# A Nyström attention with two expert layers: C v per head, blocks of 512 in the second layer, attention steps spaced

## The chip, the cores and the metric

The program runs on one core of a Trainium2 chip, in one launch. The metric is device time in microseconds. The core has five engines that run side by side, each with its own queue of instructions: PE (TensorE, matrix products), DVE (VectorE), ACT (ScalarE), POOL (GpSimd), and SP (SyncE), which here only issues DMAs. An instruction waits in its queue until the semaphores it names are set, and everything behind it on that engine waits with it.

## The reference

```
for the 8 heads of each of 4 batches (S = 576 tokens, 64 columns, m = 32 landmarks):
    q_lm, k_lm = means of 18 neighbouring tokens
    A  = softmax(q k_lm^T / 8);  Bm = softmax(q_lm k_lm^T / 8);  C = softmax(q_lm k^T / 8)
    Z  = Bm^T / (norm1(Bm) * norminf(Bm) + 1e-6)
    six times:  Z = 2 Z - Z Bm Z
    attn = A Z C v
x = attn as (2304 tokens, 512)
h = x @ w_in   (512 x 2048);  g = h * sigmoid(h);        x = g @ w_out   (layer 1)
h = x @ w_in2;                g = h * tanh(log1p(e^h));  out = g @ w_out2  (layer 2)
```

## The kernel before

**Products.** Nearly every product of the two layers is made of three matmuls on operands that are split into a high and a low part: high times high, high times low, low times high.

**Attention.** The 8 heads of a batch go in two groups of 4 heads; a group of a batch is a unit, and there are 8 units. In a unit, `cp` (line 356) transposes C by PE, `nb` gives the norms, and `cv` (line 372) is C v. Six tiles of 96 tokens are summed; for each there are two matmuls, one for a pair of heads, of 64 rows of C by 128 columns of v. So a pair computes C of either head times v of either head, and half of the result is of no use. The useful half is picked on DVE: `s2r` (line 388) is a mask times the scale, `vt` (390) takes one 64-column half, and `rv` (391) adds the other. Then six Newton rounds follow (`nw`, line 421, with `rv` and `rb` evictions). At last `u` (line 524) gives the attention's output times layer 1's weights, in eight column tiles of 32 side by side, and `uw` (541, 544) splits it.

**Opening, 0 to about 181 us.** The attention of batches 0 and 1 and the blocks 0 and 1 of layer 1 (`ha`, `ya`) are put in order by a planner, which is given a cost on an engine for each step (`Step([("pe", 1.6)])`).

**Layer 1, about 181 to 470 us.** The 2304 tokens are 8 blocks of 288, the 2048 hidden columns are 16 tiles. Step t = 16 i + j computes `h` of tile j (6 matmuls), its silu on ACT, DVE and POOL, and, two steps late, `y` of step t-2 (12 matmuls into four banks). At the turn of two blocks, four evictions `yo` (687 on ACT, 689 on DVE) free the four banks for the next block's first `y`. The attention of batches 2 and 3 is fed in as a background generator by `advance()`, called twice a step with 1.35 credits. The weights of layer 2 are converted in the background too (`rawt`, `ct`, lines 593 to 600). Here the framework's scheduler sets the order.

**Layer 2, about 470 to 886 us.** 6 blocks of 384 tokens, 16 steps each, in the order written (`manual_schedule` for ACT, DVE and PE). Step t runs `hh` (12 matmuls of 384 columns), the mish of it, and the out products of step t-2: `o` (line 1106), 3 chunks of 128 tokens by 3 matmuls of 512 columns. `hh` has three banks, `o` the other five. The mish is, on DVE, `e`, `n`, `e`, then `z` three times; on ACT two exponentials, a logarithm and the cast to the high part `g`; on POOL the low part `g` (1050). After a block's last out product `out_block` (1064 to 1077) negates each chunk into a buffer `ot`, of which there are three, and SP stores it by two DMAs. All evictions are on ACT, except in the last block.

## Time and profile before

| what | value |
|---|---|
| median of 3 runs | 889.91 us (886.08, 889.91, 894.31) |
| profiled execution | 887.88 us, its span 886.1 us |
| PE busy | 851.9 us, 96% of the span |
| DVE, ACT, POOL busy | 648.5, 475.5, 290.3 us |
| mean granted PE clock | 0.983 of full speed |

The span is the time from the first to the last instruction that the profiler saw; the profiled execution's own time has 1.8 us more around it. Busy shares are means over all stages. A row of the timeline is a run of instructions of one kind, with the idle time just before it and what ended that in brackets. PE's matmuls overlap one another, so the row of a single matmul is longer than the distance between two starts; distances between starts are the price of one.

### The profile page before, as it was taken

How to read it: one execution, taken by the hardware profiler on the slowest of the kernel's cores; microseconds unless marked ns; L12 is line 12 of the kernel's file. 1: busy time of each engine (PE TensorE's matmuls, PEld its weight loads, DVE VectorE, ACT ScalarE, POOL GpSimd, SP SyncE). 2: the span in 40 equal slices, each digit the busy share in tenths (PEclk: the TensorE clock that was granted, in tenths of full speed). 3: DMA queues.
4: the chain of work that ended last, by engine and by line, in shares of the span. 5: the costliest groups of instructions: out<-in, count | busy, mean ns of one | idle time of the engine just before them, and what ended most of it. 6: DMA issues, size and time to landing. Idle time of an engine off the chain costs nothing.

```text
span 886.1 us, 15069 instructions
## 1 busy us (share of the span) xinstructions
PE 851.9 (96%) x5424; PEld 740.1 (84%) x5424; DVE 648.5 (73%) x1289; ACT 475.5 (54%) x1045; POOL 290.3 (33%) x331
## 2 busy tenths in 40 slices
PE   6889999999999898999999999999999999999997
PEld 5656777769998797889899889999998998998996
DVE  3878878778586868743565987787787787787776
ACT  4657555355445555654565555555555455555543
POOL 1311323034433446534333432232242242242221
PEclk8779999999999999999999999999999999999999
DMA  8735475344363466812551111000110110000000
GB/s 229 200 98 147 155 211 155 70 125 97 97 141 116 115 212 221 274 52 73 171 169 56 51 27 26 20 28 18 27 27 12 34 28 5 32 1 1 36 1 36
DMA packets 95355, 79.63 MB, mean 90 GB/s; under 512 B 52528, under 2 KB 80688, under 8 KB 95280
## 3 DMA queue, kind: packets, MB, share of 16 engines
q1 hardware_dynamic: 95280, 78.67, 30.8%
q8 instruction: 42, 0.69, 0.3%
q14 instruction: 33, 0.27, 0.1%
HBM read 60.82 MB, written 17.83 MB: 89 GB/s over the span
## 4 chain that ended last, share of the span: by engine, by line
PE 74%; DVE 8%; issue 5%; POOL 4%; ACT 4%; DMA 3%; SPq 1%; POOLq 0%; DVEq 0%; ACTq 0%
PE hh L609 21%; PE o L1106 21%; PE y L609 11%; PE h L609 5%; PE ya L835 5%; PE ha L635 4%; POOL g L667 2%; PE u L524 2%; DMA q<-in_q_dram 2%; PE nw L421 2%; DVE z L1044 1%; PE cv L372 1%; DVE rawt L596 1%; POOL rawt L591 1%; SPq L201 1%
## 5 line engine op out<-in xcount | busy, mean ns | idle before, releaser
L1050 POOL TENSOR_TENSOR g<-z,g 128x384 fp32r<-128x384 f32 x94 | 95.9, 1020 | 258.8 <-ACT g L1047 256.5
L1106 PE MATMUL o<-wh,g 128*128 128x512 f32 x576 | 166.3, 396 | 2.7 <-ACT g L1047 1.5
L609 PE MATMUL y<-g,wh 128*128 128x288 f32 x768 | 163.0, 302 | 5.6 <-POOL g L667 1.8
L609 PEld LDWEIGHTS y<-g,wh 128*128 128x128 f32 x768 | 124.5, 190 | 15.2 <-ACT th L664 4.1
L667 POOL TENSOR_TENSOR g<-g,g 128x288 fp32r<-128x288 f32 x96 | 81.2, 846 | 169.6 <-ACT g L666 140.3
L609 PE MATMUL hh<-yh,wi2h 128*128 128x384 f32 x384 | 130.4, 339 | 0.0
L609 PE MATMUL hh<-yh,wi2l 128*128 128x384 f32 x384 | 129.6, 338 | 0.0
L609 PE MATMUL hh<-yl,wi2h 128*128 128x384 f32 x384 | 129.5, 337 | 0.0
L1106 PEld LDWEIGHTS o<-wh,g 128*128 128x128 f32 x576 | 106.4, 188 | 23.5 <-ACT g L1047 3.7
L1047 ACT CAST g<-z 128x384 fp32r<-128x384 f32 x96 | 49.3, 514 | 132.2 <-DVE z L1046 132.2
L609 PE MATMUL y<-g,wl 128*128 128x288 f32 x384 | 114.0, 297 | 0.0
L1033 DVE TENSOR_SCALAR e<-hh 128x384 f32<-128x384 f32 x96 | 53.5, 557 | 69.3 <-PE hh L609 69.1
L609 PE MATMUL h<-ath,uw 128*128 128x288 f32 x384 | 95.2, 302 | 1.1 <-DVE uw L544 1.1
L1106 PE MATMUL o<-wl,g 128*128 128x512 f32 x288 | 82.2, 393 | 0.0
L1034 ACT ACTIVATE e<-e 128x384 f32<-128x384 f32 x96 | 50.3, 524 | 55.2 <-DVE e L1033 54.7
L665 DVE SCALAR_TENSOR_TENSOR g<-th,h 128x288 f32<-128x288 f32 x96 | 42.9, 447 | 50.4 <-ACT th L664 48.1
L609 PEld LDWEIGHTS hh<-yh,wi2h 128*128 128x128 f32 x384 | 72.1, 188 | 4.1
L609 PEld LDWEIGHTS hh<-yl,wi2h 128*128 128x128 f32 x384 | 72.1, 188 | 3.9
L609 PEld LDWEIGHTS y<-g,wl 128*128 128x128 f32 x384 | 72.7, 189 | 0.4 <-issue 0.4
L609 PEld LDWEIGHTS h<-ath,uw 128*128 128x128 f32 x384 | 67.4, 189 | 5.8 <-issue 3.6
L1044 DVE SCALAR_TENSOR_TENSOR z<-z,r 128x384 f32<-128x384 f32 x96 | 69.8, 727 | 3.3
L609 PEld LDWEIGHTS hh<-yh,wi2l 128*128 128x128 f32 x384 | 72.0, 188 | 0.0
(163 smaller groups left out, 1591.7 us busy)
## 6 DMA issues: line engine op xcount, KB each, us to landing
rawi<-in_moe_w_in_dram SPq DMA_DIRECT2D x16, 512.0 KB, 4.9
rawo<-in_moe_w_out_dram SPq DMA_DIRECT2D x16, 512.0 KB, 3.6
rawt<-in_moe_w_in_dram SPq DMA_DIRECT2D x16, 512.0 KB, 4.8
w2c<-ct SPq DMA_DIRECT2D x32, 256.0 KB, 2.6
rawt<-in_moe_w_out_dram SPq DMA_DIRECT2D x16, 512.0 KB, 4.4
w2r<-w2c SPq DMA_DIRECT2D x32, 256.0 KB, 2.8
v<-in_v_dram SPq DMA_DIRECT2D x32, 144.0 KB, 2.9
ysc<-yo SPq DMA_DIRECT2D x32, 144.0 KB, 1.8
```

Of the source, the lines that this page charges most:

```text
L421: pe.matmul(nbk[:, i, a : w + D], lhs, rv[:, i, a:], start=True, stop=True)
L609: pe.matmul(o, a, b_, start=first and i == 0, stop=last and i == n - 1)
L635: pe.matmul(hb[:, :HB], uw[j // 2][:, g, j % 2], ath[0][:, g, hf * HB : (hf + 1) * HB], start=g == 0, stop=g == 1)
L665: dve.scalar_tensor_tensor(g2, th, 1.0, hb[:, :HB], op0=ALU.add, op1=ALU.mult)
L667: eng.tensor_tensor(gl, g2, gh.bitcast(F32), op=ALU.subtract)
L835: pe.matmul(yb[hf, m][:, :HB], wof[j][:, m * P : (m + 1) * P], gst[j // 2][:, j % 2, hf], start=j == 0, stop=j == NF - 1,)
L1033: dve.tensor_scalar(e, h, 20.0, None, op0=ALU.min)
L1034: ins = act.activation(e, e, AF.Exp)
L1044: dve.scalar_tensor_tensor(z, z, -2.0, r, op0=ALU.add, op1=ALU.mult)
L1047: act.copy(gh, z)
L1050: eng.tensor_tensor(gl, z, gh.bitcast(F32), op=ALU.subtract)
L1106: pe.matmul(obank[i][c], a[:, c * P : (c + 1) * P], w, start=j == 0 and k == 0, stop=j == NF - 1 and k == 2,)
```

## The change

Three things are changed. First, `cv` is computed per head, in four column tiles of 32 that stand side by side: 24 matmuls of 64 columns in place of 12 of 128, and one DVE instruction scales the result into `rv`. `s2r`, `vt` and the mask `sel2` with its 5 POOL memsets are gone; the planner's costs for the two steps are lowered. Second, layer 2 goes in five blocks, three of 512 tokens and two of 384; a block of 512 has four chunks. `ot` has two buffers, and where there are four chunks the evictions alternate between ACT and DVE. At j = 0 the out products go chunk by chunk. Larger buffers (`BIG`) make some others move: `g` of layer 2 into other buffers, and 14 of the 16 low tiles of layer 2's input weights in pairs into the buffers of layer 1's weights. Third, `advance()` issues at most one step on PE at a call, keeps no more than 4 credits, and gives no credit away for a step without cost; at a turn of two blocks of layer 1 the first of the two calls is left out and the second, after `y`, gets twice the credits.

```diff
-NB2 = 384
+NB2 = (512, 512, 512, 384, 384)
+BIG = max(NB2)
...
-        yield Step([("pe", 1.6)], ...
+        yield Step([("pe", 1.2)], ...
...
         for r in range(S // PT):
-            for p in range(2):
+            for h in range(4):
                 pe.matmul(
-                    cv[64 * p : 64 * p + 64, :P].rearrange("a (h d) -> a h d", h=2),
-                    ct[r // 3][:, r % 3, 64 * p : 64 * p + 64],
-                    st["v", p][:, :, r, :],
+                    cv[32 * h : 32 * h + 32, :D],
+                    ct[r // 3][:, r % 3, 32 * h : 32 * h + 32],
+                    st["v", h // 2][:, h % 2, r, :],
                     start=r == 0,
                     stop=r == S // PT - 1,
                 )
-        yield Step([("dve", 2.1)])
+        yield Step([("dve", 1.6)])
...
-        s2r = ap.tile([P, 2], F32, tag="s2r", bufs=2, name=f"s2r{u}")
-        dve.tensor_scalar(s2r, sel2, rc[:, 1:2], n2[:, 3:4], op0=ALU.mult, op1=ALU.mult)
-        vt = ap.tile([P, D], F32, tag="lk", bufs=2, name=f"vt{u}")
-        dve.tensor_scalar(vt, cv[:, :D], s2r[:, 0:1], None, op0=ALU.mult)
-        dve.scalar_tensor_tensor(rv[:, i, -D:], cv[:, D:P], s2r[:, 1:2], vt, op0=ALU.mult, op1=ALU.add)
+        dve.tensor_scalar(rv[:, i, -D:], cv[:, :D], rc[:, 1:2], n2[:, 3:4], op0=ALU.mult, op1=ALU.mult)
...
-    def advance(n=1.0):
-        credit[0] += n
-        while credit[0] >= 1:
-            credit[0] -= 1
-            while bg:
-                try:
-                    next(bg[0])
-                    break
-                except StopIteration:
-                    bg.pop(0)
+    pend = {}
+
+    def advance(n=1.0, all=False):
+
+        credit[0] = min(credit[0] + n, 4.0)
+        begun = False
+        while bg and (credit[0] >= 1 or all):
+            gen = bg[0]
+            if gen not in pend:
+                pend[gen] = next(gen, None)
+            step = pend.pop(gen)
+            if step is None:
+                bg.pop(0)
+                continue
+            on_pe = bool(step.cost) and step.cost[0][0] == "pe"
+            if on_pe and begun and not all:
+                pend[gen] = step
+                break
+            pend[gen] = next(gen, None)
+            if step.cost:
+                credit[0] -= 1
+                begun = True
+            if on_pe and not all:
+                break
...
-                    if j < 11:
+                    if j < 2:
                         lo = pl.tile([P, ND, P], F32R, tag=f"lo{j}", name=f"wi2l{j}")
                     else:
-                        lo = wp.tile([P, ND, P], F32R, tag=f"g{j - 11}", name=f"wi2l{j}")
+                        if j % 2 == 0:
+                            los = wp.tile([P, 2, ND, P], F32R, tag=f"g{j // 2 - 1}", name=f"wi2l{j}")
+                        lo = los[:, j % 2]
...
-        advance(RB)
+        turn = t > LAG and (j - LAG) % NF in (NF - 1, 0)
+        if not turn:
+            advance(RB)
...
         if t >= LAG:
             emit_y(t - LAG)
-        advance(RB)
+        advance(2 * RB if turn else RB)
...
     def out_block(i):
-        for c in range(NCH):
-            ot = m2.tile([P, DM], F32, tag="ot", bufs=3, name=f"ot{i}_{c}")
-            if i < nblk - 1 or c == 0:
+        for c in range(NB2[i] // P):
+            ot = m2.tile([P, DM], F32, tag="ot", bufs=2, name=f"ot{i}_{c}")
+            if c == 0 or i < nblk - 1 and c == 2:
                 act.mul(ot, obank[i][c], -1.0)
-            elif c == 1:
+            elif c == 1 or i < nblk - 1:
                 dve.tensor_scalar(ot, obank[i][c], -1.0, None, op0=ALU.mult)
...
+        chunks = NB2[i] // P
         if j == 0:
-            obank[i] = [bank((NCH * i + c + 4) % 5, f"o{i}_{c}") for c in range(NCH)]
-        order = [(c, k) for k in range(3) for c in range(NCH)]
+            obank[i] = [bank((sum(NB2[:i]) // P + c + 4) % 5, f"o{i}_{c}") for c in range(chunks)]
+        order = [(c, k) for k in range(3) for c in range(chunks)]
+        if j == 0:
+            order = [(c, k) for c in range(chunks) for k in range(3)]
```

DVE in layer 1, where the attention of batch 2 and the conversion of weights meet (`uw` splits the attention's product, `rawt` and `ct` are weights, `g` the silu, `lm` the landmarks). Before:

```order
L286 TENSOR_REDUCE lm_3574<-qT_3575 128x32
L596 SCALAR_TENSOR_TENSOR rawt_3848<-rawt_3848 128x512
L596 SCALAR_TENSOR_TENSOR rawt_3957<-rawt_3957 128x512
L665 SCALAR_TENSOR_TENSOR g_3406<-th_3405,h_3397 128x288
L600 SCALAR_TENSOR_TENSOR ct_4104<-rawt_3848 128x512
L544 TENSOR_TENSOR uw_5_3421<-u_3411,uw_5_3421 128x256
L544 TENSOR_TENSOR uw_5_3421<-u_3412,uw_5_3421 128x256
```

Now:

```order
L285 TENSOR_REDUCE lm_3740<-qT_3741 128x32
L539 TENSOR_TENSOR uw_6_3534<-u_3524,uw_6_3534 128x256
L539 TENSOR_TENSOR uw_6_3534<-u_3525,uw_6_3534 128x256
L591 SCALAR_TENSOR_TENSOR rawt_4111<-rawt_4111 128x512
L591 SCALAR_TENSOR_TENSOR rawt_4239<-rawt_4239 128x512
L660 SCALAR_TENSOR_TENSOR g_3566<-th_3565,h_3557 128x288
```

The `uw` pair stands ahead of the two `rawt`, no longer behind them and `ct`.

PE at the turn from block 4 to block 5 of layer 1 (`y_3` ends the old block, `y_0` opens the new one). Before:

```order
L609 MATMUL y_3_3296<-g_288_3879,wl_14_1828 128x288
L609 MATMUL h_3992<-ath_2153,uw_1_3022 128x288
L609 MATMUL h_3992<-atl_2154,uw_1_3022 128x288
L609 MATMUL h_3992<-ath_2153,uw_1_3022 128x288 x2
L609 MATMUL h_3992<-atl_2154,uw_1_3022 128x288
L609 MATMUL h_3992<-ath_2153,uw_1_3022 128x288
L356 MATMUL cp_4007<-ident,ce_3842 96x128 x3
L609 MATMUL y_0_4011<-g_288_3917,wh_0_1522 128x288 x2
```

Now:

```order
L604 MATMUL y_3_3293<-g_288_3896,wl_14_1856 128x288
L604 MATMUL h_4023<-ath_2165,uw_1_3037 128x288
L604 MATMUL h_4023<-atl_2166,uw_1_3037 128x288
L604 MATMUL h_4023<-ath_2165,uw_1_3037 128x288 x2
L604 MATMUL h_4023<-atl_2166,uw_1_3037 128x288
L604 MATMUL h_4023<-ath_2165,uw_1_3037 128x288
L604 MATMUL y_0_4037<-g_288_3933,wh_0_1566 128x288 x2
```

The attention's `cp` no longer stands between `h` and the new block's first `y`.

ACT at the first turn of two blocks in layer 2, with the semaphores that each instruction waits for (DMAHW is a DMA, the others are engines). Before:

```order
L1041 ACTIVATE r_6521<-r_6521 128x384 [waits Activation_49]
L1069 ACTIVATE ot_0_6544<-o_0_5932 128x512 [waits PE_49]
L1069 ACTIVATE ot_1_6548<-o_1_5933 128x512 [waits DMAHW0_49,PE_49]
L1069 ACTIVATE ot_2_6552<-o_2_5934 128x512 [waits DMAHW3_49,PE_49]
L1034 ACTIVATE e_6569<-e_6569 128x384 [waits DVE_49]
```

Now, ACT and then DVE at the same turn:

```order
L1060 ACTIVATE r_6618<-r_6618 128x512 [waits Activation_49]
L1088 ACTIVATE ot_0_6644<-o_0_5983 128x512 [waits DMAHW0_49,PE_49]
L1088 ACTIVATE ot_2_6652<-o_2_5985 128x512 [waits DMAHW4_49,DMAHW5_49,PE_49,Activation_49]
L1053 ACTIVATE e_6673<-e_6673 128x512 [waits DVE_49]
```

```order
L1058 TENSOR_TENSOR e_6616<-n_6617,hh_6603 128x512 [waits DVE_49]
L1090 TENSOR_SCALAR ot_1_6648<-o_1_5984 128x512 [waits DMAHW3_49,PE_49]
L1090 TENSOR_SCALAR ot_3_6656<-o_3_5986 128x512 [waits DMAHW6_49,DMAHW7_49,DVE_49,PE_49]
L1052 TENSOR_SCALAR e_6673<-hh_6660 128x512 [waits PE_49]
L1062 SCALAR_TENSOR_TENSOR z_6619<-n_6617,r_6618 128x512 [waits Activation_49,Pool_49]
```

Two evictions stand on ACT and two on DVE, the second of each behind its engine's first and behind the two DMAs that empty the buffer it writes; `e` of the next step stands behind them on both engines.

## Rows read from the trace of the kernel before

**Rows 1.** The page, busy time per engine: us, share of the span, instructions.

```profile
PE 851.9 (96%) x5424; PEld 740.1 (84%) x5424; DVE 648.5 (73%) x1289; ACT 475.5 (54%) x1045; POOL 290.3 (33%) x331
```

**Rows 2.** Busy time by stretch of the span: length, each engine's us, granted clock, DMA.

```profile
185.00:470.00 285.00, 273.80 (x2222) 251.87 (x2223) 184.11 (x407) 154.42 (x372) 124.09 (x140) 0.99 0.49 143
...
507.00:863.00 356.00, 356.00 (x1779) 321.36 (x1778) 282.24 (x511) 189.89 (x374) 106.85 (x104) 1.00 0.07 21
```

**Rows 3.** Waits of PE: what for, us in total, times, longest us.

```profile
PE h L609 <- DVE uw L544: 1.1, 1, 1.1
```

**Rows 4.** Chain of waits, middle of layer 2: start us, us, engine, line, instructions.

```profile
579.54 2.08 PE o L1106 x9
581.63 2.11 PE hh L609 x12
```

**Rows 5.** Timeline of PE: start us, us, engine, line, operation, out<-in, shapes, count.

```profile
214.93 1.53 PE L372 MATMUL cv<-v,ct 96*64 96x128 f32 x24
...
266.77 0.72 PE L524 MATMUL u<-wc,wt 64*32 64x256 f32 x16
```

**Rows 6.** The instructions of line 372: duration ns min/median/max.

```profile
L372 PE MATMUL cv<-v,ct x192: 272/273/476, 32.5 to 347.1; 96*64 96x128 f32 x192
```

**Rows 7.** Chain of waits, attention of the first batch.

```profile
32.53 1.71 PE cv L372 x24
...
41.53 0.21 DVE s2r L388
...
41.84 0.29 DVE vt L390
```

**Rows 8.** Timeline of PE and DVE near 296 us; in brackets idle before, releaser.

```profile
298.60 0.59 PE L356 MATMUL cp<-ident,ce 128*96 128x128 f32 x3 [2.32 <-DVE uw L544]
...
295.58 1.44 DVE L596 SCALAR_TENSOR_TENSOR rawt<-rawt 128x512 uint32<-128x512 uint32 x2
...
298.14 0.74 DVE L544 TENSOR_TENSOR uw<-u,uw 128x256 fp32r<-128x256 f32 x2
```

**Rows 9.** Busy time by stretch, after that wait.

```profile
299.00:302.50 3.50, 3.50 (x17) 3.50 (x16) 0.72 (x2) 1.32 (x3) 0.33 (x1) 0.52 0.71 214
```

**Rows 10.** Timeline of PE, turn from block 4 to block 5 of layer 1.

```profile
339.61 0.60 PE L609 MATMUL y<-g,wh 128*128 128x288 f32 x2 [0.84 <-DVE yo L689]
...
341.39 0.53 PE L609 MATMUL y<-g,wh 128*128 128x288 f32 x2 [1.05 <-ACT yo L687]
```

**Rows 11.** Timeline of PE, first out products of layer 2.

```profile
480.81 0.50 PE L1106 MATMUL o<-wh,g 128*128 128x512 f32 x1 [0.28 <-DVE yo L689]
481.88 0.50 PE L1106 MATMUL o<-wh,g 128*128 128x512 f32 x1 [0.57 <-ACT yo L687]
```

**Rows 12.** Timeline of PE, out products in the first block of layer 2.

```profile
494.34 0.96 PE L1106 MATMUL o<-wh,g 128*128 128x512 f32 x3
...
498.93 0.96 PE L1106 MATMUL o<-wh,g 128*128 128x512 f32 x3
```

**Rows 13.** Chain of waits, then timeline: first turn of two blocks in layer 2.

```profile
547.99 2.11 PE hh L609 x12
550.11 2.17 PE o L1106 x9
...
549.76 1.56 ACT L1069 ACTIVATE ot<-o 128x512 f32<-128x512 f32 x3
...
550.37 3.12 SPq L1077 DMA_DIRECT2D out_dram<-ot  x6
```

**Rows 14.** DMA issues: out<-in, engine, count, KB each, median us to landing.

```profile
out_dram<-ot SPq DMA_DIRECT2D x9, 256.0 KB, 2.3
```

**Rows 15.** DVE by line and shape: busy us, mean ns, idle before.

```profile
L1071 DVE TENSOR_SCALAR ot<-o 128x512 f32<-128x512 f32 x1 | 0.7, 691 | 1.2 <-PE o L1106 1.2
```

**Rows 16.** Timeline, end of the program.

```profile
881.69 1.51 SPq L1077 DMA_DIRECT2D out_dram<-ot  x3
882.00 0.39 ACT L1074 ACTIVATE ot<-o 128x256 f32<-128x256 f32 x1 [0.33 <-PE o L1106]
```

More of the change, by code (lines that the diff above doesn't have):

```diff
@@ L122, in nystrom_moe_kernel @@
     mask4 = cp.tile([P, 4], F32, name="mask4")
-    sel2 = cp.tile([P, 2], F32, name="sel2")
     blk = cp.tile([P, P], F32, name="blk")
     two = cp.tile([P, 1], F32, name="two")
-    for t in (mask2, mask4, sel2, blk):
+    for t in (mask2, mask4, blk):
         pool.memset(t, 0.0)
@@ L358, in attn_unit @@
             act.copy(ct[hf].rearrange("a r m -> a (r m)"), pt[:PT, : 3 * P])
-        yield Step([("pe", 1.6)], [("ld", b, g, "v", p) for p in range(2)] if perm else (), ("cv", b, g))
+        yield Step([("pe", 1.2)], [("ld", b, g, "v", p) for p in range(2)] if perm else (), ("cv", b, g))
         nb = atbank(f"nb{u}")
@@ L909, in y_load @@
     def y_load(i, pl):
-        yh = pl.tile([P, ND, NB2], F32R, tag=f"yh{i % 2}", bufs=1, name=f"yh{i}")
-        yl = pl.tile([P, ND, NB2], F32R, tag=f"yl{i % 2}", bufs=1, name=f"yl{i}")
+        yh = pl.tile([P, ND, BIG], F32R, tag=f"yh{i % 2}", bufs=1, name=f"yh{i}")
+        yl = pl.tile([P, ND, BIG], F32R, tag=f"yl{i % 2}", bufs=1, name=f"yl{i}")
+        w, at = NB2[i], sum(NB2[:i])
+        yh, yl = yh[:, :, :w], yl[:, :, :w]
         raws = []
@@ L960, in gtiles @@
     def gtiles(t, n):
-        gt_ = wp.tile([P, 2, n], F32R, tag=f"gt{t % 3}", name=f"g{t}_{n}")
-        return gt_[:, 0], gt_[:, 1]
+        if "tail" not in late:
+            gt_ = wp.tile([P, 2, HB], F32R, tag=f"gt{t % 3}", name=f"g{t}_{n}")
+        elif t % 3 == 2:
+            gt_ = wp.tile([P, 2, BIG], F32R, tag="g7", name=f"g{t}_{n}")
+        else:
+            gt_ = late["tail"].tile([P, 2, BIG], F32R, tag=f"gz{t % 3}", bufs=1, name=f"g{t}_{n}")
+        return gt_[:, 0, :n], gt_[:, 1, :n]
     def emit_y(t):
@@ L977, in nystrom_moe_kernel @@
         if hf == 1 and b + 1 < B and j == SHIFT + 1:
-            while bg:
-                advance()
+            advance(0, True)
             if b + 2 < B:
@@ L997, in nystrom_moe_kernel @@
             u_all(b, lin // 2)
-        advance(RB)
+        turn = t > LAG and (j - LAG) % NF in (NF - 1, 0)
+        if not turn:
+            advance(RB)
         if i < nblk - 1:
-            while cvn[0] < min(34, (18 * (t - 11) // 52 if t < 64 else t - 45)):
+            while not turn and cvn[0] < min(34, (18 * (t - 11) // 52 if t < 64 else t - 45)):
                 cvn[0] += 1
@@ L1075, in out_block @@
                 dve.tensor_scalar(ot[:, h:], obank[i][c][:, h:], -1.0, None, op0=ALU.mult)
-            for r0, r1, rows in out_rows(i * NB2 + c * P):
+            for r0, r1, rows in out_rows(sum(NB2[:i]) + c * P):
                 sp.dma_start(rows, ot[r0:r1])
@@ L1122, in nystrom_moe_kernel @@
                 hb = bank(5 + t % 3, f"hh{t}")
-                h_matmuls(hb, win2[j], ys[i], NB2)
-                mish[t] = mish_steps(t, hb[:, :NB2])
+                h_matmuls(hb, win2[j], ys[i], NB2[i])
+                mish[t] = mish_steps(t, hb[:, : NB2[i]])
                 next(mish[t])
```

24 lines of the change are left out of this document (12 added, 12 removed).

## The prediction

> **What bounds the kernel.** The page's busy times come first: PE works 851.9 us of the span of 886.1, and the next engine, DVE, 648.5 [rows 1]. Then the table by stretches, since that share is a mean: in layer 2 PE has no idle time at all between 507 and 863 us, at the full clock, while DVE is busy 282.24 of 356.00 us, or 79%; in layer 1, from 185 to 470 us, PE works 273.80 of 285.00 us [rows 2]. So there is no slack to win in the middle of layer 2 but fewer or shorter matmuls, and 11.2 us of gaps in layer 1. The list of waits then tells what the gaps are, and the timeline where each lies. Any wait that the change makes on PE is paid in full.
>
> All sums are made against the profiled execution, 887.88 us; the median is 889.91, so 2.0 us above it, and I add that at the end.
>
> **C v per head.** One unit's `cv`, 12 matmuls that the trace shows in two parts each, is 24 instructions in 1.53 us [rows 5]. The last of them lasts 0.273 [rows 6], and two stand side by side in two column tiles, so twelve pairs start about 0.11 us apart. Now there are 48, in twelve sets of four side by side, and each has half the columns. The row nearest to this is `u`: sixteen matmuls of 256 columns, eight tiles side by side, in 0.72 us [rows 5], so many narrow tiles do run beside each other. If the time goes by columns, a unit saves half of 1.53 - 0.27, that is 0.63 us; if four tiles start no denser than two, nothing. I take 0.63, as the `u` row speaks for it, with 0 as the other end. Five of the 8 units lie where PE is the bound: 3.15 us. The Trainium skill, "TensorE: Matmul & The Clock Gate", Part 1, section "Wait — 56ns, not 53.3ns?", says that two matmuls never start closer than about 25 ns; by that, as an estimate, the 48 starts of a unit would take 1.2 us, and most of the saving would be gone. The `u` row has starts closer than one in 45 ns on average with its loads in between, and doesn't decide it.
>
> In the first batch the attention itself is the chain. `cv` lies on it with 1.71 us, and later, in the second unit, `s2r` and `vt` with 0.21 and 0.29 [rows 7]. Some 0.65 of the first, and both of the others, go: 0.65 + 0.50 = 1.15 us. The 5 POOL memsets are on no chain that I saw and count nothing; the other units' two DVE instructions are hidden by PE's own work.
>
> **The planner's order.** The lowered costs move whole pieces of the opening. Where it ends, PE waits 1.1 us for `uw` ahead of the first `h` [rows 3]; in the new order two more `u` are covered by `ya` products, so I count 1.1 us gained. What the rest of the reordering does between 50 and 180 us I can't read; ±2 us in the range.
>
> **Attention steps spaced.** The longest wait of layer 1 is one of 2.32 us: `cp` waits for `uw`, which stands on DVE behind two `rawt` of 1.44 us and a `ct` [rows 8]. Behind it the granted clock is 0.52 for 3.5 us [rows 9], the lower of the two levels, 1.2 GHz; that is half of 3.4 us or 1.7 us lost. In the new order `uw` stands ahead of the `rawt`, so I take all of it as gained: 2.3 + 1.7 = 4.0 us. At the turn of block 4 to 5, `y` waits 0.84 and 1.05 us for `yo` [rows 10]. The new order has `cp` gone from that place, and with it, on DVE, the attention's and converter's instructions ahead of the first `yo`: 1.9 us gained. But the steps kept from a turn come later, and all that remain are drained at one place near a block's end, in closer order; there Newton rounds wait on `rv` evictions already. I give back 1.0 us, about half of what the turn gains (my choice; between 0 and the whole 4.9). Net 4.9 us.
>
> In the last block of layer 1 the low weight tiles of layer 2 must wait for layer 1's weights to be done with, from j = 2 and not 11; their splits on DVE stand closer together and ahead of silu. PE has little idle there now; I take 0.5 us lost, 0 to 1.5.
>
> First part: 3.15 + 1.15 + 1.1 + 4.9 - 0.5 = 9.8 us gained.
>
> **Blocks of 512.** A steady step is 2.11 us of `hh` and 2.08 of `o` [rows 4]: 0.176 us for each of 12 matmuls of 384 columns, and 0.231 for each of 9 of 512. A 512 step is 24 of the latter, 5.55 us (2.08 x 24 / 9). Before, 96 steps of 4.19: 402.2 us. Now 48 of 5.55 and 32 of 4.19: 400.3. So 1.9 us gained. It is so little because the columns stay the same; only 192 matmuls' fixed share, some 10 ns each, goes. DVE, ACT and POOL work grows with the columns as PE's does, so they stay at about 80% or less.
>
> The first `o` of layer 2 waits for `yo` evictions, two starts 1.07 us apart where 0.231 would do, and 0.28 before that [rows 11]. A chunk-by-chunk order and `hh` of 2.8 us ahead of it cover these: 1.1 us (0.84 + 0.28). Five turns cost 0.09 us each (2.17 against 2.08) [rows 13, 4]; 0.45. In the first block's steps, `o` starts 4.59 us apart, not 4.19 [rows 12]; with four such steps 1.6 us are lost there. A 512 step has more room around whatever holds them up; I take half, 0.8. Sum: 1.9 + 1.1 + 0.45 + 0.8 = 4.25 us gained.
>
> **Two buffers for four evictions.** This is the loss. Before, at a turn, ACT's three evictions take 0.52 us each, the first done 2.3 us after the last `o` of the block (549.76 + 0.52, against 547.99 where `hh` follows that `o`), and SP issues six DMAs, 0.52 us apart [rows 13]; a store has landed 2.3 us after issue [rows 14]. PE waits for none of it [rows 2]. After the change chunk 2 on ACT must wait until chunk 0's two stores have landed, and chunk 3 on DVE until chunk 1's. With steps of 5.55 us, counted from the end of the old block's last `o`: chunk 0 evicted at 2.8, its stores landed at about 5.5, chunk 2 evicted at 6.1. PE runs `hh` to 2.8 and reaches chunk 3 of the next block's first `o`, which needs chunk 2's bank, at 4.85: it waits 1.2. Chunk 3 is evicted on DVE (0.69 us each [rows 15]) at 7.2, and behind it stand `e` of the next step and the three `z` that make `g`: some 2.8 us with the cast 0.6 behind them, 10.6. PE needs `g` at 9.6 (6.75 and a `hh` of 2.8): 1.1 more. So 2.35 us at each of three turns, the one into 384 included, and 0.2 at the last: 7.3 us.
>
> At the end, the halves of the last chunk need chunk 0's buffer too. Its store is issued at 881.69, and the eviction began at 882.00 [rows 16]; 881.69 + 2.3 = 884.0: 2.0 us later. Together 9.3 us lost, with 0 and, by the slower rival below, 21 as the ends.
>
> **Sum.** 9.8 + 4.25 - 9.3 = 4.75 us gained: 887.88 - 4.75 = 883.13, and with the 2.03 us up to the median 885.2.
>
> **Rivals.**
> - *The turns cost nothing* (0.20): stores land early enough, or `g` has more lead, so 7.3 us aren't lost: 877.9. For it: at the turn of before `o` runs on in spite of 1.56 us of evictions on ACT. Against it: the order lists the stores among what the evictions wait for.
> - *Spacing gives nothing back* (0.16): waits for `uw` and `yo` move to other steps, and the drained ones wait for their own evictions. Without the 4.9: 890.1. For it: PE does the same attention work beside the same DVE load; against it: the 2.32 us are due to three DVE instructions that now stand elsewhere.
> - *Slower: the stores become the bound at the turns* (0.13). Stores of two engines' evictions are issued in one queue, 0.52 us apart, beside the loads of `y`. If they land in 4 and not 2.3 us, each turn and the end lose 1.7 us more, 6.8 in all; and once the wait comes in one piece as long as the 2.3 us of layer 1 the clock may halve behind it, 1.7 us at each of three turns, 5.1: 897.1. It decides from a landing of about 4 us on.
> - *The narrow tiles of `cv` give nothing* (0.02, as the `u` row bears it out): 3.15 us less gained, 888.3. This is the case to which the skill's rule on starts would lead.
>
> The forecast has 0.49; its own range is 880 to 891, from the ends of the planner's order, the last block and the drained steps. Runs of before spread over 8 us; one per cent, about 9 us, is what a measurement of this kernel can tell from no change. Faster by over 1% means under 881.0: most of the first rival (0.17) and the low end of the forecast (0.13), 0.30. Slower means over 898.8: the slower rival where it also loses the spacing, and something of the others, 0.10. The rest, 0.60, is within 1%. The range that holds 8 in 10 goes from 876 to 896.
>
> **What would show it.** In the changed kernel's trace: `cv` runs of about 0.9 us; no wait of `cp` for `uw` over 1 us, and no stretch at 0.52 in layer 1; `y` without waits for `yo` at turns; `o` and `hh` steps of 2.77 us; at three turns a wait of `o` for `ot` near 1.2 us and one for `g` near 1.1, and on ACT and DVE idle time ended by the stores; the last eviction near 2 us later behind the last `o`. The forecast is wrong if the turns lose under 1 or over 4 us each, or if layer 1 is as long as before.

## The result: slower by 1.2%, by layer 2's stores and by the planner's order

The changed kernel takes 897.7 us (median of 8 runs, 894.92 to 900.31) against 887.85 us for the kernel before (8 runs): a ratio of 1.0117, 95% interval 1.009 to 1.0143. Forecast were 885.2 us and a range of 876 to 896. The profiled execution shown here took 900.31 us, 2.6 us above the median and the longest of the eight.

PE still works almost all the time, and its own work is a little shorter:

```profile
PE 850.1 (95%) x5424; PEld 713.5 (79%) x5424; DVE 636.4 (71%) x1184; ACT 460.5 (51%) x970; POOL 291.1 (32%) x306
```

Compared with [rows 1], PE's busy time fell by 1.8 us while the span grew by 12.4. The table by stretches tells where PE now stands still: busy us of PE is the number behind the length.

```profile
188.00:478.00 290.00, 276.01 (x2353) 252.73 (x2337) 189.79 (x404) 157.02 (x378) 126.59 (x140) 0.99 0.49 144
507.00:863.00 356.00, 347.68 (x1581) 293.18 (x1580) 269.40 (x421) 173.84 (x302) 105.97 (x88) 1.00 0.07 21
```

In [rows 2] the middle of layer 2 had no idle time; now 8.3 us of 356 are idle. The waits of PE name it. Columns as in [rows 3].

```profile
PE o L1128 <- ACT g L1066: 7.5, 5, 3.7
...
PE u L519 <- ACT ce L331: 2.8, 1, 2.8
...
PE o L1128 <- ACT ot L1088: 2.4, 2, 1.4
...
PE h L604 <- DVE uw L539: 1.5, 1, 1.5
```

`o` waits 7.5 us for `g` and 2.4 us for `ot`; before, it waited 1.5 us for `g` and never for `ot`. The wait of `cp` for `uw` [rows 8] is gone, and `u` waits 2.8 us for ACT in its place. `h` waits 1.5 us for `uw` where the opening ends; before, it was 1.1 us [rows 3]. Behind the waits of `h` and of `u` the granted clock is at the lower of its two levels, 1.2 GHz:

```profile
192.80:196.20 3.40, 3.40 (x15) 2.35 (x12) 2.83 (x5) 0.99 (x3) 1.83 (x2) 0.50 0.41 67
308.80:312.20 3.40, 3.40 (x16) 3.40 (x16) 3.40 (x9) 2.02 (x5) 2.73 (x4) 0.51 0.58 174
```

A count by three stages helps, from PE's timeline: the opening up to the first `h`, layer 1 from there to the first `hh`, layer 2 from there to the end. All are single profiled executions.

| kernel | median us | opening | layer 1 | layer 2 |
|---|---|---|---|---|
| before | 887.85 | 181.15 | 289.39 | 415.53 |
| changed | 897.7 | 188.45 | 289.33 | 420.74 |
| difference | +9.9 | +7.30 | -0.06 | +5.21 |
| forecast of it | -4.75 | -2.9 | -6.9 | +5.05 |

The forecast by stages is the sum of the prediction's terms, with one of the five units of C v counted to the opening. Layer 2 came out as forecast; the opening and layer 1 did not.

**Layer 2's turn.** Timelines of the changed kernel at the first turn, ACT, DVE and PE: the last `o` of the old block ends where `hh` starts, at 575.61.

```profile
577.77 0.58 ACT L1088 ACTIVATE ot<-o 128x512 f32<-128x512 f32 x1
580.88 0.60 ACT L1088 ACTIVATE ot<-o 128x512 f32<-128x512 f32 x1 [2.53 <-DMA out_dram<-ot]
...
585.72 0.62 ACT L1066 CAST g<-z 128x512 fp32r<-128x512 f32 x1 [1.48 <-DVE z L1065]
```

```profile
577.08 0.69 DVE L1090 TENSOR_SCALAR ot<-o 128x512 f32<-128x512 f32 x1
582.29 0.69 DVE L1090 TENSOR_SCALAR ot<-o 128x512 f32<-128x512 f32 x1 [4.53 <-DMA out_dram<-ot]
```

```profile
575.61 0.39 PE L604 MATMUL hh<-yh,wi2h 128*128 128x512 f32 x1
...
581.53 0.50 PE L1128 MATMUL o<-wh,g 128*128 128x512 f32 x1 [0.99 <-ACT ot L1088]
```

Counted from 575.61: chunk 0 is evicted at 2.7 us (forecast 2.8), chunk 2 at 5.9 (6.1) after 2.53 us of waiting for a store, chunk 3 at 7.4 (7.2) after 4.53 us of waiting; `o` waits 0.99 us for chunk 2 (1.2), and `g` is cast at 10.7 (10.6). The two steps of this turn take 6.72 and 6.96 us where 5.44 is the rule, so 2.8 us are lost (2.35). The chain of waits of this stretch goes by the store that the second eviction on DVE waits for:

```profile
577.77 0.59 ACT ot L1088
...
579.80 2.36 DMA out_dram<-ot
...
582.29 0.09 DVE ot L1090
```

The second turn loses 3.0. The third, from 512 to 384, loses 5.5 instead of 2.4, in one piece:

```profile
765.94 1.39 PE L1128 MATMUL o<-wh,g 128*128 128x512 f32 x3 [3.69 <-ACT g L1066]
```

```profile
765.90:769.60 3.70, 3.66 (x9) 2.94 (x10) 3.34 (x7) 2.13 (x5) 1.10 (x2) 0.55 0.00 0
```

Here a wait of 3.69 us is followed by 3.7 us at a mean granted clock of 0.55, most of it at the lower level: three `o` take 1.39 us where they took 0.86 or so. Late stores are the smaller part of what differs from the first turn:

```profile
755.80 0.33 PE L604 MATMUL hh<-yh,wi2h 128*128 128x384 f32 x1
...
762.49 0.69 DVE L1090 TENSOR_SCALAR ot<-o 128x512 f32<-128x512 f32 x1 [5.38 <-DMA out_dram<-ot]
...
765.38 0.51 ACT L1066 CAST g<-z 128x384 fp32r<-128x384 f32 x1 [1.18 <-DVE z L1065]
```

Counted from 755.80, where `hh` follows the old block's last `o`, chunk 3 is evicted at 7.4 us and `g` is cast at 10.1, much as at the first turn (7.4 and 10.7), though chunks 0 and 1 are evicted some 0.9 us earlier; so much longer do their stores take. But PE's own work until it needs that `g` is now two `hh` of 384 columns and one `o` step of three chunks. It is done after 6.45 us; at the first turn it was 9.6, the wait for `ot` included. So nearly all of the delay falls on PE in one wait.

How long the two other turns are also differs between executions. In after_oldcost (below), whose layer 2 is the same, `o` waits longer for `ot` at the first and second turn, and the clock falls behind both (0.62 and 0.64 in the 4 us from 572 and from 664 us):

```profile
572.31 0.50 PE L1128 MATMUL o<-wh,g 128*128 128x512 f32 x1 [2.34 <-ACT ot L1088]
...
664.07 0.50 PE L1128 MATMUL o<-wh,g 128*128 128x512 f32 x1 [2.51 <-ACT ot L1088]
```

At the end, the last chunk's halves wait for chunk 0's store:

```profile
892.00 0.60 ACT L1088 ACTIVATE ot<-o 128x512 f32<-128x512 f32 x1 [1.51 <-PE o L1128]
...
892.62 3.34 SPq L1096 DMA_DIRECT2D out_dram<-ot  x3
894.76 0.38 ACT L1093 ACTIVATE ot<-o 128x256 f32<-128x256 f32 x1 [2.17 <-DMA out_dram<-ot]
```

From the start of chunk 0's eviction to that of the halves it is 2.76 us; before it was 0.93 (881.07 in the row below to 882.00 [rows 16]). That is 1.8 us later (2.0).

```profile
881.07 0.60 ACT L1069 ACTIVATE ot<-o 128x512 f32<-128x512 f32 x1 [1.51 <-PE o L1106]
```

**C v.** One unit of the changed kernel in PE's timeline:

```profile
224.93 0.88 PE L371 MATMUL cv<-v,ct 96*32 96x64 f32 x48
```

0.88 us against 1.53 [rows 5]: 0.65 us a unit, as forecast (0.63). The last matmul of a run lasts 0.22 us:

```profile
L371 PE MATMUL cv<-v,ct x384: 219/219/317, 32.8 to 362.7; 96*32 96x64 f32 x192
```

So the 48 starts lie within 0.66 us, 14 ns apart on average.

### The profile page after: what moved, and what is told of

It is laid out like the page before. It is cut to its first block, busy times and chain, and to the rows that moved or that the text cites. A ratio compares the mean times of both kernels' runs of the same rounds, so it can differ in the third digit from the quotient of the medians.

```text
span 898.5 us, 14782 instructions
## 1 busy us (share of the span) xinstructions
PE 850.1 (95%) x5424; PEld 713.5 (79%) x5424; DVE 636.4 (71%) x1184; ACT 460.5 (51%) x970; POOL 291.1 (32%) x306
## 4 chain that ended last, share of the span: by engine, by line
PE 72%; DVE 10%; issue 5%; DMA 4%; ACT 4%; POOL 3%; SPq 1%; DVEq 0%; ACTq 0%; POOLq 0%
PE hh L604 20%; PE o L1128 20%; PE y L604 11%; PE ya L843 6%; PE h L604 5%; PE ha L630 3%; PE u L519 2%; POOL g L662 2%; DMA q<-in_q_dram 2%; PE nw L416 1%; DMA out_dram<-ot 1%; POOL rawt L586 1%; DVE rawt L591 1%; DVE z L1063 1%; DVE z L1065 1%
## 5 line engine op out<-in xcount | busy, mean ns | idle before, releaser
L1069 POOL TENSOR_TENSOR g<-z,g 128x512 fp32r<-128x512 f32 (+1 forms) x78 | 92.9, 1191 | 265.5 <-ACT g L1066 265.5
L1128 PE MATMUL o<-wh,g 128*128 128x512 f32 x576 | 162.2, 394 | 10.2 <-ACT g L1066 7.5
L604 PE MATMUL hh<-yh,wi2h 128*128 128x512 f32 (+1 forms) x320 | 118.7, 371 | 0.0
L604 PE MATMUL hh<-yh,wi2l 128*128 128x512 f32 (+1 forms) x320 | 118.7, 371 | 0.0
L604 PE MATMUL hh<-yl,wi2h 128*128 128x512 f32 (+1 forms) x320 | 118.4, 370 | 0.0
L1066 ACT CAST g<-z 128x512 fp32r<-128x512 f32 (+1 forms) x80 | 46.2, 578 | 126.4 <-DVE z L1065 125.2
L1052 DVE TENSOR_SCALAR e<-hh 128x512 f32<-128x512 f32 (+1 forms) x80 | 51.0, 637 | 72.2 <-PE hh L604 72.1
L1053 ACT ACTIVATE e<-e 128x512 f32<-128x512 f32 (+1 forms) x80 | 47.1, 589 | 67.4 <-DVE e L1052 67.3
L843 PE MATMUL ya<-gs,wl 128*128 128x288 f32 x256 | 70.2, 420 | 2.6 <-ACT yo L682 1.7
L604 PEld LDWEIGHTS hh<-yl,wi2h 128*128 128x128 f32 x320 | 60.1, 188 | 9.5
L661 ACT CAST g<-g 128x288 fp32r<-128x288 f32 x96 | 41.5, 433 | 50.2 <-DVE g L660 49.9
```

The lines of the kernel that those rows point to most:

```text
L604: pe.matmul(o, a, b_, start=first and i == 0, stop=last and i == n - 1)
L661: act.copy(gh, g2)
L843: pe.matmul(yb[hf, m][:, :HB], wof[j][:, m * P : (m + 1) * P], gst[j // 2][:, j % 2, hf], start=j == 0, stop=j == NF - 1,)
L1052: dve.tensor_scalar(e, h, 20.0, None, op0=ALU.min)
L1053: ins = act.activation(e, e, AF.Exp)
L1066: act.copy(gh, z)
```

## The experiments

Each kernel was timed in 3 rounds against the kernel before on the same chip. Names in the table: C v is the first part of the change, layer 2 the second, spacing the third. The runs were made in five groups, in which the kernel before had medians from 886.06 to 890.17 us; kernels of different groups are better compared by their ratios.

| label | parts | median us | ratio to before (95%) | opening | layer 1 | layer 2 |
|---|---|---|---|---|---|---|
| cv_alone | C v, lowered costs | 890.13 | 1.0042 (1.002 to 1.0064) | 185.33 | 288.99 | 414.08 |
| cv_oldcost | C v, old costs | 880.04 | 0.9916 (0.9891 to 0.9942) | 177.70 | 284.63 | 414.47 |
| cv_pecost | C v, PE cost lowered | 898.90 | 1.0148 (1.0111 to 1.0185) | 180.06 | 302.52 | 413.86 |
| cv_dvecost | C v, DVE cost lowered | 880.67 | 0.994 (0.9919 to 0.9961) | 178.00 | 285.89 | 414.50 |
| spacing_alone | spacing | 886.24 | 0.999 (0.9968 to 1.0011) | 179.30 | 289.46 | 415.66 |
| layer2_alone | layer 2 | 887.11 | 1.0006 (0.9983 to 1.0029) | 181.99 | 283.83 | 422.55 |
| after_oldcost | all, old costs | 892.07 | 1.0063 (1.003 to 1.0096) | 176.59 | 290.65 | 422.97 |
| after_ot4 | all, 4 out buffers | 884.13 | 0.9965 (0.9942 to 0.9989) | 186.83 | 287.65 | 407.79 |
| after_oldcost_ot4 | all, both | 878.16 | 0.99 (0.9855 to 0.9945) | 178.72 | 292.98 | 407.75 |
| cv_layer2_ot4 | no spacing, both | 870.36 | 0.9814 (0.9776 to 0.9852) | 179.81 | 280.91 | 407.77 |
| best_turn | the same, turn rule | 868.54 | 0.9791 (0.9745 to 0.9836) | 179.90 | 281.60 | 407.78 |
| best_onepe | the same, one-step rule | 871.82 | 0.9844 (0.9808 to 0.9881) | 177.44 | 284.37 | 407.80 |
| best_pause | no spacing, conversion paused | 871.22 | 0.9795 (0.975 to 0.9839) | 178.74 | 283.54 | 407.81 |
| spaced_pause | all, conversion paused | 875.95 | 0.9868 (0.9827 to 0.9908) | 176.73 | 288.81 | 407.77 |
| best_ushift | no spacing, u a step later | 875.92 | 0.9845 (0.9795 to 0.9894) | 179.60 | 285.04 | 407.80 |
| turn_ushift | turn rule, u a step later | 875.27 | 0.985 (0.9804 to 0.9895) | 181.33 | 285.55 | 407.78 |
| spaced_ushift | all, u a step later | 878.89 | 0.9888 (0.9842 to 0.9933) | 177.47 | 290.43 | 407.80 |

From after_oldcost_ot4 down, all have the old costs and four out buffers. Openings in the same planner's order differ between executions: 181.15, 179.30 and 181.99 us in the order of before.

### The three parts alone

cv_alone takes the first part with its costs:

```diff
-        yield Step([("pe", 1.6)], ...
+        yield Step([("pe", 1.2)], ...
...
-        yield Step([("dve", 2.1)])
+        yield Step([("dve", 1.6)])
```

> Only C v per head, with the planner's lowered costs; layer 2 and the feeding of attention steps as before. In the changed kernel's profile the opening ended 7.3 us later than before (first h of layer 1 at 188.45 against 181.15 us). Theory 1, the planner's new order costs it: the opening is again 5 to 7 us longer, the four later units give back some 0.6 us each, the whole is 2 to 5 us slower than before. Rival, the arrival of a load or the clock of that one execution: the opening is about 1 to 3 us shorter than before and the whole 3 to 5 us faster, as the prediction had it.

Measured: 1.0042, some 3 us slower; the opening 4.2 us longer, a little less than the 5 to 7 expected. Theory 1 stands. cv_oldcost has the same new products without these two edits.

> C v per head, with the planner's costs for its two steps left as they were (1.6 on PE, 2.1 on DVE). Theory 1 with the costs as its cause: the opening's order is nearly that of before, the first h comes 1 to 2 us earlier than before, and the whole is 3 to 5 us faster. Rival, the order suffers from the removed instructions and not from the costs: as slow as with the lowered costs, 2 to 5 us above before.

Measured: 0.9916, 7.2 us faster, more than the 3 to 5 expected. So C v per head is a good edit, and the two numbers given to the planner cost 10 us, 7.6 in the opening and 4.4 in layer 1 of the profiles. PE's waits from 55 to 188 us show part of how, with the lowered costs first and then with the old ones:

```profile
PE tr L242 <- DMA q<-in_q_dram: 2.8, 1, 2.8
...
PE ya L829 <- ACT yo L681: 1.7, 1, 1.7
...
PE ya L829 <- DVE wl L594: 1.0, 2, 0.5
```

```profile
PE tr L242 <- DMA q<-in_q_dram: 0.8, 1, 0.8
```

With the lowered costs `ya` comes to stand where its weights (`wl`) and its evictions (`yo`) aren't ready, and the transposes of `q` ahead of the load. In these 133 us PE works 124.16 us at a mean granted clock of 0.96 with the lowered costs, and 129.82 us at 0.99 with the old ones. The planner's costs only set an order, and a cost nearer to the measured one gave a worse order here.

spacing_alone takes the third part, all edits of the change in `advance` and around its calls:

```diff
-    def advance(n=1.0):
+    def advance(n=1.0, all=False):
...
+        turn = t > LAG and (j - LAG) % NF in (NF - 1, 0)
```

> Only the spaced attention steps. In the changed kernel layer 1 took as long as before (289.3 us from the first h to the first hh in both), though four units of C v were shorter by some 0.6 us each. Theory 1, the waits only moved and the drained steps of the last batch cost a little more: 1 to 3 us slower than before. Rival, the forecast's 4.9 us gain is real and something else took it back: 4 to 5 us faster.

Measured: 0.999, no change; layer 1 289.46 against 289.39 us. Neither expectation holds to the letter, the first is nearer. The wait of `cp` for `uw` is gone, as the prediction had it, while at the turn `y` still waits 1.4 us where it waited 1.9. By the starts of `h`, the spaced kernel is 6.4 us ahead at the 56th step of layer 1, though a part of that is attention work that it has put off. At the 64th step it is 0.8 us behind. In between, what is left of the attention is drained, and `nw` waits for `rv` there:

```profile
356.82 1.21 PE L421 MATMUL nw<-rv,rb 128*128 128x96 f32 x3 [2.61 <-DVE rv L395]
```

```profile
356.30:363.20 6.90, 6.38 (x27) 6.21 (x28) 4.63 (x12) 3.76 (x8) 3.50 (x5) 0.51 0.71 244
```

That is 2.6 us of waiting, and some 3.4 us (half of 6.9) lost to the lower clock level around it: about 6 us where the prediction gave back 1.0.

layer2_alone takes the second, with all that depends on it:

```diff
-NB2 = 384
+NB2 = (512, 512, 512, 384, 384)
...
-            ot = m2.tile([P, DM], F32, tag="ot", bufs=3, name=f"ot{i}_{c}")
+            ot = m2.tile([P, DM], F32, tag="ot", bufs=2, name=f"ot{i}_{c}")
```

> Only the second layer's blocks of 512 and 384 with two buffers for the four evictions. Theory 1, stores that the evictions wait for cost 2.6 to 3 us at each of two turns, 5.5 at the third, and 2 at the end: layer 2 as in the changed kernel, 5 us longer than before, and the whole 4 to 6 us slower. Rival, the layer 2 loss hung on what came before it: 1 us or less.

Measured: 1.0006. Layer 2 is 7.0 us longer, as theory 1 says, but layer 1 is 5.6 us shorter, which no theory had. Some 3 us of it lie in layer 1's last block and just ahead of it. By the starts of `h`, the time from the 76th step to the first `hh` is 51.4 to 52.9 us in the six traces with the old layer 2, and 48.8 to 50.6 in the thirteen with the new one. In the kernel before, `y` waits there 1.67 us for `g`, and PE works 20.02 us of the stretch from 414 to 436 us; in layer2_alone it works 21.66 of the same 22 us.

```profile
435.67 0.50 PE L609 MATMUL y<-g,wh 128*128 128x288 f32 x2 [1.67 <-ACT g L666]
```

```profile
414.00:436.00 22.00, 20.02 (x147) 19.42 (x146) 10.29 (x18) 12.98 (x30) 10.70 (x12) 1.00 0.55 157
```

```profile
414.00:436.00 22.00, 21.66 (x163) 21.43 (x162) 8.63 (x16) 12.69 (x30) 13.12 (x13) 1.00 0.47 140
```

The splits of layer 2's weights are what the second part moves there; which of them made the difference was not singled out. The rest lies mainly near 300 us, where in this execution the clock stayed full behind a shorter wait of `cp` (1.60 us).

### The two losses undone in the whole change

after_oldcost is the whole change with the planner's costs left as they were (here and below the diffs are against the changed kernel, where nothing else is said):

```diff
-        yield Step([("pe", 1.2)], ...
+        yield Step([("pe", 1.6)], ...
...
-        yield Step([("dve", 1.6)])
+        yield Step([("dve", 2.1)])
```

> The whole change, but with the planner's costs left at 1.6 and 2.1. Theory 1, the lowered costs lose some 7 us in the opening (first h at 185.33 against 177.70 us with C v alone): first h at 177 to 180 us, the whole 7 to 10 us under the changed kernel, 887 to 891 us. Rival, the opening of the changed kernel suffers from something else in the combination: within 2 us of the changed kernel, 896 to 899.

Measured: 892.07 us, 5.6 under the changed kernel, a little less than expected; the opening is 176.59 us, 11.9 shorter in these profiles, of which layer 1 and 2 give back some (layer 2 by the two longer turns shown above). after_ot4 has four buffers for the evictions:

```diff
-            ot = m2.tile([P, DM], F32, tag="ot", bufs=2, name=f"ot{i}_{c}")
+            ot = m2.tile([P, DM], F32, tag="ot", bufs=4, name=f"ot{i}_{c}")
...
-        n = m2.tile([P, BIG], F32, tag="n", bufs=2, name=f"n{t}")[:, :w]
+        n = m2.tile([P, BIG], F32, tag="e" if t == len(steps) - 1 else "n", bufs=3 if t == len(steps) - 1 else 1, name=f"n{t}")[:, :w]
```

> The whole change, with four buffers for the out evictions in place of two (one buffer of the mish's n given up for them; DVE's own order keeps n safe). Theory 1, the waits for stores cost all of the excess at the turns (2.7, 3.0 and 5.5 us in the changed kernel's profile) and 2 us at the end: layer 2, from the first hh to the end, falls from 420.7 to 408 to 411 us, the whole to 885 to 889. Rival, what holds PE at the turns is the two evictions on DVE and their order on that engine, with stores in their shadow: layer 2 stays above 416 us.

Measured: layer 2 407.79 us, 12.95 less, and 884.13 us in all, a little more than expected. Theory 1 stands: no step at a turn is longer than its neighbours, and the last evictions stand as close as before:

```profile
877.36 0.60 ACT L1088 ACTIVATE ot<-o 128x512 f32<-128x512 f32 x1 [1.51 <-PE o L1128]
...
878.28 0.39 ACT L1093 ACTIVATE ot<-o 128x256 f32<-128x256 f32 x1 [0.33 <-PE o L1128]
```

The middle of layer 2, in the same combination without spacing, has no idle time again:

```profile
507.00:838.00 331.00, 331.00 (x1523) 281.59 (x1523) 256.42 (x408) 165.56 (x289) 97.76 (x81) 1.00 0.07 20
```

after_oldcost_ot4 has both of these edits, and cv_layer2_ot4 leaves out the spacing (all edits of spacing_alone) as well.

> The whole change with both mended: the planner's costs as before, four buffers for the out evictions. If the two losses are independent, the gains add: 7 to 10 us and 10 to 12 us under the changed kernel, 876 to 880 us. If layer 1's order answers to each edit by itself, some us more on either side.

> C v per head with the old costs and layer 2 in blocks of 512 with four buffers; attention steps fed as before. Theory 1, spacing gave back nothing: as fast as the whole change with both mended, within 2 us, 874 to 880. Rival, the spacing hides what the other parts need: 3 us or more above it.

Measured: 878.16 and 870.36 us. The first is as expected. The second is what neither theory had: without spacing it is 7.8 us faster, and layer 1 takes 280.91 instead of 292.98 us. (The profiled execution of the first took 881.23 us, the longest of its four, so the two profiles lie 11 us apart.)

### Why the spacing costs layer 1

The two rules of the spacing one by one, as edits to cv_layer2_ot4: in best_turn the lines with `turn`, in best_onepe the new `advance`.

```diff
+        turn = t > LAG and (j - LAG) % NF in (NF - 1, 0)
+        if not turn:
+            advance(RB)
...
+        advance(2 * RB if turn else RB)
```

```diff
+            if on_pe and begun and not all:
+                pend[gen] = step
+                break
```

> C v per head with the old costs, layer 2 with four buffers, and of the spacing only the turn: the first call of advance left out there, the second doubled. The whole spacing made this combination 7.8 us slower (878.2 against 870.4). Theory 1, the one PE step per call is what lines up u behind cp and pushes the last batch's steps on: with the turn alone 869 to 872. Rival, the turn's doubled credits bunch the steps: 875 or more.

> The same, but of the spacing only advance's new rule (one PE step a call, at most 4 credits, steps without cost free), no special case at turns. Theory 1: as slow as the whole spacing, 876 to 880, with u waiting on ACT some 2 us near the 40th step of layer 1. Rival: 869 to 872, and the turn is to blame.

Measured: 868.54 and 871.82 us. The turn rule does no harm, as theory 1 says; but the one-step rule alone does little either, so neither theory holds: only both together cost some 8 us. cv_pecost and cv_dvecost take the planner's two costs one by one, as edits to cv_oldcost: the first `1.6` to `1.2` on PE, the second `2.1` to `1.6` on DVE.

> C v per head, only the cost on PE lowered (1.2), the one on DVE left at 2.1. With both lowered 890.1, with neither 880.0. If the PE cost reorders the opening: near 890 with the first h at 184 us or later. If not: near 880.

> C v per head, only the cost on DVE lowered (1.6), the one on PE left at 1.6. Its order of PE in the opening stands closer to that with both old costs: near 880 to 883, first h at 177 to 181 us. Rival, the DVE cost is the harmful one: near 890.

Measured: 898.90 and 880.67 us. The PE cost is the harmful one, but not as I thought: its opening is 180.06 us, and layer 1 is 302.52. With both lowered the opening pays instead. So layer 1, which the framework's scheduler orders, answers to an edit ahead of it by as much as 18 us.

What PE waits for there, in after_oldcost_ot4:

```profile
296.02 1.59 PE L519 MATMUL u<-wc,wt 64*32 64x256 f32 x16 [2.22 <-ACT ce L331]
...
309.56 0.67 PE L519 MATMUL u<-wc,wt 64*32 64x256 f32 x14 [1.75 <-ACT ct L357]
```

```profile
296.00:354.00 58.00, 52.96 (x425) 47.66 (x426) 44.40 (x94) 32.50 (x76) 30.08 (x32) 0.91 0.57 173
```

`u` waits 2.22 us for `ce`, the softmax of C, and 1.75 us for `ct`, the eviction of `cp`. From 296 to 354 us the granted clock is 0.91 on average, so some 5 us of these 58 are lost to the lower level too. All of layer 1, first in after_oldcost_ot4 and then in cv_layer2_ot4:

```profile
178.72:471.70 292.98, 278.74 (x2369) 255.39 (x2361) 189.56 (x407) 159.03 (x382) 125.94 (x140) 0.98 0.49 142
179.81:460.72 280.91, 272.62 (x2368) 251.05 (x2361) 185.59 (x407) 158.99 (x382) 126.74 (x140) 0.99 0.50 149
```

So about half of the 12.1 us between them is idle time of PE (14.2 against 8.3 us), and the other half is time in which PE works longer at the same matmuls, more of it at the lower level. I took the weight conversion on ACT and DVE for the cause, as it stands ahead of these evictions, and paused it there:

```diff
-            while cvn[0] < min(34, (18 * (t - 11) // 52 if t < 64 else t - 45)):
+            while cvn[0] < min(34, (18 * (min(t, 33) - 11) // 52 if t < 53 else t - 45)):
```

> C v per head with the old costs, layer 2 with four buffers, no spacing, and the conversion of layer 2's weights paused from the 34th to the 52nd step of layer 1's background section, then one step of it at each step. Theory 2, what PE waits for in layer 1 are evictions that stand behind the conversion's instructions on DVE and ACT: the waits of 2.9 us (cp for uw) and 2.7 us (y for g) go, with the half clock behind them; layer 1 falls from 280.9 to 273 to 277 us, the whole from 870.4 to 862 to 867. If the conversions then meet the Newton rounds, 1 to 3 us come back there. Rival, the attention's own instructions hold the evictions up: layer 1 stays within 2 us.

> The whole change with the old costs and four buffers, spacing included, and the same pause of the conversion. Without the pause 878.2 us and 293.0 us in layer 1, with u waiting 2.2 and 1.8 us for ACT. Theory 2: those waits go, layer 1 falls to 279 to 285 us, the whole to 864 to 871, and most of the difference between spaced and not spaced is gone. Rival, the spacing's own order makes u wait: layer 1 stays above 289 us.

Measured: 871.22 and 875.95 us. Neither differs from the version without the pause by more than the noise (ratios 0.9795 against 0.9814 without spacing, 0.9868 against 0.99 with it; the intervals overlap). With spacing the waits are still there:

```profile
292.54 1.14 PE L519 MATMUL u<-wc,wt 64*32 64x256 f32 x16 [1.83 <-ACT ce L331]
...
305.69 1.10 PE L519 MATMUL u<-wc,wt 64*32 64x256 f32 x14 [1.90 <-ACT ct L357]
```

Theory 2 falls as the whole cause. Without spacing `cp` does wait less (1.19 us, not 2.87) and the wait of `y` for `g` is gone, so the conversion has a part in both; but other waits came, and layer 1 is 2.6 us longer. What is left is the banks. In layer 1 PSUM has four banks for `y`, two for `h`, and two, 5 and 7, for the attention and `u` together, taken in turns (`Banks(5, 7)`). A `u` needs both. So a `u` between `c` and its softmax, or between `cp` and `ct`, waits on PE, with `h` and `y` behind it; and a `cp` behind a `u` waits for `uw`, which is the wait of 2.32 us in [rows 8]. To test it, `u` was issued a step later:

```diff
-        if b > 1 and lin < NF and lin % 2 == 0:
+        if b > 1 and lin < NF and lin % 2 == 1:
```

> The whole change with the old costs and four buffers, and in the first half of each of layer 1's batches the product u is issued one step later; nothing else. Theory 3: u and the attention's steps take turns in two PSUM banks, so a u that comes between c or cp and its eviction waits for it on PE, and a cp behind u waits for uw. The two waits of u (2.2 and 1.8 us, the conversion away 1.8 and 1.9) then move or go with one step of distance: layer 1 differs from 293.0 by 3 us or more, more likely down, 284 to 290, the whole 870 to 876. Rival, something other than the pairing of u with c and cp holds u up: the same waits stay, layer 1 within 2 us of 293.

> The same shift of u in the combination without spacing (870.4, layer 1 280.9 us, cp waiting 2.9 us for uw). Theory 3: the wait of cp for uw changes by a us or more, to either side, as u stands at another distance from it: 867 to 874. Rival: that wait stays as it is.

> The same shift with the turn rule (868.5 without the shift). 865 to 872 by theory 3; unchanged by the rival.

Measured: layer 1 2.5 us shorter, 4.1 longer and 4.0 longer; the wholes 878.89, 875.92 and 875.27 us. The first moved less than expected, the others ended 2 and 3 us above what was expected (ratios 0.9845 and 0.985, where they were 0.9814 and 0.9791 without the shift). The waits did as theory 3 says. Without spacing, where `cp` waited for `uw` (first row, cv_layer2_ot4), it is now `u` that waits for `ct` (second, best_ushift):

```profile
296.88 0.59 PE L355 MATMUL cp<-ident,ce 128*96 128x128 f32 x3 [2.87 <-DVE uw L539]
```

```profile
297.72 0.66 PE L519 MATMUL u<-wc,wt 64*32 64x256 f32 x14 [2.03 <-ACT ct L357]
```

With spacing `u` no longer waits for `ct`, and `cp` waits for `uw`:

```profile
306.51 0.58 PE L355 MATMUL cp<-ident,ce 128*96 128x128 f32 x3 [1.87 <-DVE uw L539]
```

That the waits around the 40th step go through the two shared banks is shown by the kernel, in which nothing else ties `cp` to `uw`, and by these exchanges; that they make up all of the 12 us between spaced and not spaced is not. By the starts of `h`, after_oldcost_ot4 is level with cv_layer2_ot4 at the 40th step, 5.2 us behind at the 60th and 11.2 at the 64th. In that last stretch its remaining Newton rounds are drained, as in spacing_alone: `nw` waits 1.92 us for `rv`, with the lower clock behind it, and a part of the stretch is attention work that the other kernel had done before. Why only both rules together bring `u` into a bad place is the scheduler's order, which stays open. A third pair of banks, which would settle the size, wasn't tried: all eight are taken.

## Why the prediction was wrong, point by point

- **C v per head** was right: 0.65 us a unit (0.63). In the rows of `cv` above, 48 starts lie within 0.66 us, 14 ns apart on average. The Trainium skill, "TensorE: Matmul & The Clock Gate", Part 1, section "Wait — 56ns, not 53.3ns?", has starts never closer than about 25 ns; side by side in four column tiles the trace shows them closer, and the measurement decides. The trace of the kernel before already had it: the starts of its two `cv` matmuls side by side are 6 to 7 ns apart.
- **The planner's order** is the first step that failed. The prediction read that order at one place, counted 1.1 us gained, and put "±2 us in the range" for what it could not read. The lowered costs lose 10 us: cv_alone against cv_oldcost, 890.13 and 880.04. The 1.1 us themselves didn't come either: that wait is 1.5 us now, with the lower clock behind it. The mistake was not in a duration; an order with new waits was priced as if it kept the old ones.
- **Attention steps spaced** is the second: "I take all of it as gained: 2.3 + 1.7 = 4.0 us". The wait of `cp` did go from its place, as forecast, and in the changed kernel all but 0.5 us of the ones for `yo`. The term that failed is the 1.0 us given back for the drained steps: with the spacing alone they cost about 6 us, and the gain is gone. In the changed kernel `u` waits 2.76 us where `cp` did, with half the clock behind it. And the row's cause was read only in part: `uw` was late for `cp` behind the conversion on DVE, but `cp` needed it at all since both go through one pair of banks (with the conversion paused, `cp` still waits 1.2 of 2.9 us without spacing, and `u` 1.8 and 1.9 with it). So a new order moves the wait to another pair. This is the rival "spacing gives nothing back", to which I gave 0.16.
- **The last block** was forecast to lose 0.5 us; with the new layer 2 some 3 us are gained there.
- **Blocks of 512** gave more than the 4.25 us forecast: with four buffers layer 2 takes 407.8 instead of 415.5 us, 7.7 less. A 512 step takes 5.53 or, in the second block, 5.44 us, not 5.55, and a 384 step of the last block 4.16 and not 4.19; over 80 steps this is 2.7 of the 3.5 us more.
- **Two buffers for four evictions** was right in its mechanism, chunk by chunk within 0.3 us at the first turn. Its size was 12.95 us and not 9.3, and some 15 us by layer2_alone and after_oldcost (422.55 and 422.97 us against 407.8). "2.35 us at each of three turns, the one into 384 included" is the term that was too small: into 384, PE's own work covers 6.45 us and not 9.6, so 3.7 us of waiting come in one piece, the clock halves behind it, and 5.5 us are lost. The slower rival had priced that halving as 1.7 us a turn, with a store landing in 4 us as its condition. In the changed kernel the stores of two sizes did land later than the 2.3 and 1.9 us of before, but at the two other turns the waits stayed short. In after_oldcost the clock fell at all three turns, without a median landing near 4 us (2.0 to 3.0 us for the four sizes). That rival's 897.1 us lies beside the measured 897.7 by luck: layer 2 came out as forecast, and the loss lies in the opening and layer 1.

```profile
out_dram<-ot SPq DMA_DIRECT2D x6, 192.0 KB, 3.5
...
out_dram<-ot SPq DMA_DIRECT2D x6, 64.0 KB, 3.3
```

As a whole, layer 2 was forecast within 0.2 us by two errors that cancel, 3.5 us too little gained and 3.7 too little lost. The 17.2 us between the sum's 883.1 and the profiled execution's 900.3 lie in the opening (10.2) and layer 1 (6.9).

The best of the versions is C v with the old costs and layer 2 with four buffers, with or without the turn rule: 868.54 us (ratio 0.9791, 0.9745 to 0.9836) and 870.36 us (0.9814, 0.9776 to 0.9852), 27 to 29 us under the changed kernel. Between the two no difference is shown, nor to the one with the conversion paused (0.9795).

## What to carry to other kernels

A wait names the buffer's last reader; ask first which buffer two pieces of work share, since moving one of them then moves the wait instead of removing it. Before a pool loses a buffer, count who must be done with it, down to the store's landing, and lay out each kind of turn chunk by chunk, with PE's own work as the cover: in the profiled execution the one turn laid out came within a few tenths of a us, and the other kind, which was not, was missed by 3 us. Work that is put off to clear one place has to be paid where it is drained; lay out that place too. Where a planner or scheduler sets the order, change its costs in a run of their own.
